# Half-width score tiles with one exponential per head, an expand moved ahead of two DMA issues, and a selection matrix in place of transposes

## The chip, the cores and the metric

The kernel runs on one core of a Trainium2 chip. The metric is the device time of one execution in microseconds. Four runs of the kernel before took 6482.04 to 6499.41 us, with a median of 6487.83 us.

## What is computed

The reference is a forward pass and its gradients. Two attention branches read the same 2048 tokens of width 576:

```python
q = (x @ wq) in 32 heads of 18;  k = x @ wk;  v = x @ wv      # branch A: one k and v for all heads
a = softmax(q k^T * 18**-0.5) v, heads joined, @ wo
mem = mem0                                                    # branch B: 64 segments of 32 tokens
for s in range(64):
    h = concat([mem, x[segment s]])                           # 8 memory rows and 32 tokens
    q, k, v = h @ Wq, h @ Wk, h @ Wv                          # 32 heads of 128
    o = softmax(masked q k^T * 128**-0.5) v, heads joined, @ Wo
    mem, out[s] = o[:8], o[8:]
b = concat(out);  g = sigmoid((x * gate_w).sum(-1))
result = g * a + (1 - g) * b
```

The outputs are this result and the gradients of ten inputs and weights for a given gradient of the result. What matters here: the memory of branch B makes its segments a chain (backward too), and branch A's scores are 2048 x 2048 for each of 32 heads, computed once in the forward half and again in the backward half.

## The kernel before, in words

The kernel is a row of stages: setup and projections, a forward weave, the bulk of branch B's attention, a backward weave, and the weight gradients at the end. The edits lie in the two weaves.

A weave (`weave`, L211) alternates, in an order that is written out by hand, one piece of branch B's chain (a Python generator, up to its next `yield`) with one step of branch A's sweep. There are 64 segments with 16 pieces each and 1024 steps, so each piece is followed by one step. No scheduler moves anything: on each engine, instructions stand in the order in which the code issues them. Every engine works through its own queue in that order and waits at the first instruction that is not ready.

**The forward sweep** is `a_pass1` (L1372). A step n handles two heads, 128 keys and 512 queries. PE gets, in this order: S of step n+1 (two matmuls with 32 rows each, `mm_S`, L1385), dP of step n (two matmuls, L1419), the accumulation of W of step n-1 (four matmuls, L1426) and of E of step n (four, L1435). ACT gets the exponential of step n+1 (`ex`, L1392), DVE gets two products W = dP * E of step n (L1424), one per head. S is one tile of two banks, held once; dP has two tiles of one bank, one per head. So S of the next step waits until ACT has read the whole S tile, and each dP waits until DVE has read the dP of the same head of the step before.

**The backward sweep** is `a_pass2` (L1499), with the same loop: `mm_S` (L1526), dP (L1548), `ex` (L1530), two products (L1553), and four accumulations of the step before, two with dS and two with E (L1561).

**The forward chain** is `b_chain_fwd` (L237). A segment's pieces are: two halves of the k projection; transpose of the memory rows of k (`mem_T`, L231, then a copy on ACT, L308); two halves of q; transpose of q (copy on DVE, L334); first half of v; scores and exponential (L342 to L353); denominators (L355 to L359); second half of v, with the normalised probabilities `c_pn` on DVE (L366) and their expansion to block form `c_PB` on POOL (L369); transpose of v; the output `po` from `c_PB` (L375 to L379), with a cast to `c_oT` on DVE (L381); and four pieces that multiply by Wo and form the next memory. POOL also issues DMAs: in the second v piece it issues the store of v's rows (`rows_out`, L364) and of `c_pn` (L367) ahead of the expansion. SP later reads v's rows back (`rows_copy`, L300).

**The backward chain** is `b_chain_bwd` (L793), 16 pieces a segment as well. It uses `mem_T` once a segment (L856), with a copy on ACT (L858). It already uses `seln` (L136, a 128x32 matrix of zeros and ones that picks the eight memory rows out of each 32) as a moving operand at L913 and L924.

`mem_T` is given rows in [128, 8, 128] with the memory rows of four groups of heads at partitions 0 to 7, 32 to 39, 64 to 71 and 96 to 103. It makes eight full 128x128 transposes into a bf16 tile and hands on a strided view of the 32 useful columns of each.

Of the kernel before, what the change touches and what calls it, by code (L numbers as in the profile page):

```python
# [6 lines left out]
ACT = mybir.ActivationFunctionType  # L7
ALU = mybir.AluOpType
AX = mybir.AxisListType
BF16 = mybir.dt.bfloat16  # L10
F32 = mybir.dt.float32
P = 128
# [13 lines left out]
SCALEA = float(DA) ** -0.5  # L26
# [4 lines left out]
class Kern:  # L31
# [197 lines left out]
        return pj  # L229

    def mem_T(self, t2, psum, tag, bufs):  # L231
        pt = psum.tile([P, 8, P], BF16, name=tag, bufs=bufs)
        for u in range(8):
            self.tr(pt[:, u, :], t2[:, u, :], P)
        return pt[:].rearrange("p u (c t) -> p u c t", t=32)[:, :, :, 0:8]

    def b_chain_fwd(self, keep, sp, psum):  # L237
        nc = self.nc
# [21 lines left out]
        def load_k(s):  # L260
            kx = sp.tile([P, HB, 32], BF16, name="c_kx", bufs=1)
            nc.sync.dma_start_transpose(kx[:], self.xtok["k"][s * 32:(s + 1) * 32, :])
            return kx
# [23 lines left out]
        for s in range(NSEG):  # L287
            h_ = hm[s % 2]
            nc.gpsimd.dma_start(self.memT_dram[:, :, s, :], h_[:, :, 0:8])
            t2 = {w: sp.tile([P, 8, E], BF16, name=f"c_{w}2", bufs=1) for w in ("k", "q", "v")}  # L290
# [6 lines left out]
            def rows_out(w):  # L297
                nc.gpsimd.dma_start(self.row_dram[w][s], t2[w][:].rearrange("p u e -> p (u e)"))

            def rows_copy(w):  # L300
                src = self.row_dram[w][s].rearrange("(c r) e -> c r e", r=32)
                t0, n = ride(s)
                nc.sync.dma_start(self.mtok[w][s * 8:(s + 1) * 8, :].rearrange("r (c e) -> c r e", c=4), src[:, 0:8, :])
                if n:
                    nc.sync.dma_start(self.xtok[w][t0:t0 + n, :].rearrange("r (c e) -> c r e", c=4), src[:, 8:8 + n, :])
# [42 lines left out]
            for u in range(8):  # L348
                for c in range(4):
                    self.mm(ps[32 * c:32 * c + 8, 64 + 8 * u:72 + 8 * u], lhsT=mT["k"][:, c, u, :],  # L350
                            rhs=qT[:, u, c, :], start=False, stop=True, tp=(0, 32 * c))
# [9 lines left out]
            proj("v", 1)  # L361
            if s + 1 < NSEG:
                kx = load_k(s + 1)
            rows_out("v")  # L364
            pn = sp.tile([P, 2, 64], BF16, name="c_pn", bufs=1)
            nc.vector.tensor_tensor(out=pn[:], in0=Et[:], in1=rd[:].unsqueeze(1).to_broadcast([P, 2, 64]), op=ALU.mult)  # L366
            nc.gpsimd.dma_start(self.pm_dram[s], pn[:].rearrange("p a b -> p (a b)"))  # L367
            PB = sp.tile([P, 16, 4, 8], BF16, name="c_PB", bufs=1)
            self.expand(PB[:], pn[:].rearrange("p a (u q) -> p (a u) q", q=8), 16)  # L369
            yield  # L370
            rows_copy("q")
            src = self.mem_T(t2["v"], psum, "c_pj", 1)
# [13 lines left out]
            if s + 1 < NSEG:  # L386
# [23 lines left out]
                for lo, hi in ((0, 256), (256, 512), (512, 576), (576, 576)):  # L410
                    if hi > lo:
                        ph = half(lo, hi)
                    if lo:
# [4 lines left out]
                        r = 64 if lo == 576 else P  # L418
# [953 lines left out]
    def a_pass1(self, keep, sp, psum, xps):  # L1372
        nc = self.nc
        T, NTT = self.T, self.NTT
        NB = NPR * (T // 512)
        dl_all = keep.tile([P, NTT, NPR, 2, 2], BF16, name="a_dl")
        QD, S, E_, W_ = {}, {}, {}, {}

        def load(b):
            if b < NB:  # L1380
                p, qb = b // 4, b % 4
                QD[b] = sp.tile([P, 512], BF16, name="a_QD", bufs=3)
                nc.sync.dma_start(QD[b][:], self.qd_dram[p][:, qb * 512:(qb + 1) * 512])

        def mm_S(n):  # L1385
            S[n] = psum.tile([P, 2, 512], F32, name="a_S", bufs=1)
            kt = n % 16
            for i in range(2):
                r = slice(32 * i, 32 * i + 32)
                self.mm(S[n][:, i, :], lhsT=self.KV[r, kt * P:kt * P + P], rhs=QD[n // 16][r, :], tp=(32 * i, 0))  # L1390

        def ex(n):  # L1392
            E_[n] = sp.tile([P, 2, 512], BF16, name="a_E", bufs=2)
            nc.scalar.activation(E_[n][:], S.pop(n)[:], ACT.Exp, scale=SCALEA)  # L1394

        def acc_mm(acc, n, src, st, first, last):
            t = src.pop(n) if src is W_ else src[n]
            for g in range(4):
                self.mm(acc[32 * g:32 * g + 32, :], lhsT=st[:, n % 16, 32 * (g % 2):32 * (g % 2) + 32],
                        rhs=t[:, g // 2, :], start=first, stop=last, tp=(0, 32 * g))  # L1400

        load(0)
        load(1)
        mm_S(0)
        ex(0)
        NP_ = 16 * NB
        acc = None
        post = None
        for n in range(NP_ + 1):
            if n < NP_:  # L1410
                kt = n % 16
                if kt == 8:
                    load(n // 16 + 2)
                if n + 1 < NP_:
                    mm_S(n + 1)
                dP = [psum.tile([P, 512], F32, name="a_dP", bufs=2) for _ in range(2)]
                for i in range(2):
                    r = slice(64 + 32 * i, 96 + 32 * i)
                    self.mm(dP[i][:], lhsT=self.KV[r, kt * P:kt * P + P], rhs=QD[n // 16][r, :], tp=(64 + 32 * i, 0))  # L1419
                if n + 1 < NP_:  # L1420
                    ex(n + 1)
                W_[n] = sp.tile([P, 2, 512], BF16, name="a_W", bufs=2)
                for i in range(2):
                    nc.vector.tensor_tensor(out=W_[n][:, i, :], in0=dP[i][:], in1=E_[n][:, i, :], op=ALU.mult)  # L1424
            if n > 0:
                acc_mm(acc, n - 1, W_, self.WK, False, n % 16 == 0)  # L1426
                if n % 16 == 0:
                    acs = sp.tile([P, 512], F32, name="a_acs", bufs=1)
                    nc.scalar.copy(acs[:], acc[:])
                    bb = n // 16 - 1  # L1430
                    post = self.a_post(bb // 4, bb % 4, acs, QD.pop(bb), sp, xps, dl_all)
            if n < NP_:
                if n % 16 == 0:
                    acc = psum.tile([P, 512], F32, name="a_acc", bufs=2)
                acc_mm(acc, n, E_, self.VK, n % 16 == 0, False)  # L1435
            if post is not None and n % 16 in (1, 4, 6):
                if next(post, "end") == "end":
                    post = None
            yield
        for _ in post:  # L1440
            pass
        for t4 in range(NTT // 4):
            ptr = xps.tile([64, 4, P], BF16, name="c_x", bufs=1)
            for j in range(4):
                self.tr(ptr[:, j, :], dl_all[:, t4 * 4 + j].rearrange("p a b c -> p (a b c)"), P)
            dlT = sp.tile([64, 512], BF16, name="a_dlT", tag="a_qt", bufs=1)
            nc.scalar.copy(dlT[:], ptr[:].rearrange("p a b -> p (a b)"))
            for p in range(NPR):
                for i in range(2):
                    nc.sync.dma_start(self.qd_dram[p][82 + 32 * i:84 + 32 * i, t4 * 512:(t4 + 1) * 512],  # L1450
                                      dlT[4 * p + 2 * i:4 * p + 2 * i + 2, :])
# [47 lines left out]
    def a_pass2(self, keep, sp, psum):  # L1499
        nc = self.nc  # L1500
# [3 lines left out]
        Q, S, E_, D_ = {}, {}, {}, {}  # L1504
# [11 lines left out]
        def pair(n):  # L1516
            return n // (NPR * NTT), n // 4, n % 4

        def mm_u(dst, n, base):
            kb, c, j = pair(n)  # L1520
            for i in range(2):
                r = slice(base + 32 * i, base + 32 * i + 32)
                self.mm(dst[i], lhsT=Q[c][0][r, j * P:j * P + P], rhs=KV[r, kb * 512:kb * 512 + 512],
                        tp=(base + 32 * i, 0))

        def mm_S(n):  # L1526
            S[n] = psum.tile([P, 2, 512], F32, name="b_S", bufs=1)
            mm_u([S[n][:, i, :] for i in range(2)], n, 0)

        def ex(n):  # L1530
            E_[n] = sp.tile([P, 2, 512], BF16, name="b_E", bufs=3)
            nc.scalar.activation(E_[n][:], S.pop(n)[:], ACT.Exp, scale=SCALEA)  # L1532

        load(0)
        load(1)
        mm_S(0)
        ex(0)
        acc = None
        NS = NPR * NTT
        NP_ = 4 * NS  # L1540
        for n in range(NP_ + 1):
# [12 lines left out]
            if n > 0:  # L1554
# [5 lines left out]
                for i4 in range(4):  # L1560
                    self.mm(acc[32 * i4:32 * i4 + 32, :], lhsT=SD[:, o % 4, 32 * i4:32 * i4 + 32],  # L1561
                            rhs=src[i4 // 2][:, i4 % 2, :],
# [236 lines left out]
```

## Time and profile before

| what | value |
|---|---|
| median of 4 runs | 6487.83 us |
| the profiled execution | 6486.87 us, of which its span is 6484.6 us |
| mean granted TensorE clock | 0.976 |
| PE busy | 5963.1 us (92% of the span) |
| DVE, ACT, POOL busy | 3772.8, 3493.8, 1962.0 us |
| forward sweep, first S to last W | 503.7 to 2456.1 us |
| backward sweep, first S to last dS | 3269.3 to 5054.4 us |
| `a_S<-...` and `b_S<-...`, 2048 matmuls each | 383 ns each |
| exponential of a whole S tile (128x1024) | 1026 and 1024 ns, 1024 of each |
| product of dP and E (128x512) | 684 and 685 ns, 2048 of each |

How to read it: the page gives busy times per engine and per group of instructions (line, engine, output tile <- input tiles). The order in time gives the start of each instruction and the idle time before it with what ended it; rows that follow each other on one engine are merged ("x2"), and then the length is that of all of them from the first start to the last end. PE overlaps matmuls, so one that is still in flight counts as busy while the next one waits. PE's starts are therefore more telling than its busy time.

### The profile page before, as it was taken

The numbers are of one execution on the slowest core, as the hardware profiler recorded it, in microseconds if no ns is written. First come the engines' busy times: TensorE is split into PE (matmuls) and PEld (weight loads), VectorE is DVE, ScalarE is ACT, GpSimd is POOL, SyncE is SP. The second block draws the span as 40 slices with busy tenths as digits, with TensorE's granted clock in tenths as the row PEclk, the third lists the DMA queues.
The fourth block names the chain that finished last, engine by engine and source line by source line (L and its number), as shares of the span: only waits on it lengthen the run. The fifth ranks groups of instructions, "written<-read, shape, count | busy, mean of one in ns | idle before, by whom it ended". The sixth has DMA issues, their size and how long they took to land. (4 is left out here: it accounts for less than half of the span.)

```text
span 6484.6 us, 208625 instructions
## 1 busy us (share of the span) xinstructions
PE 5963.1 (92%) x88611; PEld 3364.2 (52%) x88822; DVE 3772.8 (58%) x7061; ACT 3493.8 (54%) x5105; POOL 1962.0 (30%) x3451
## 2 busy tenths in 40 slices
PE   7898999999999994999969999999999899899996
PEld 5443444444444443877734444444444677675443
DVE  4336777777777773666658888888888211111111
ACT  3326777777777773666547777777677322211101
POOL 3003333333333333444423333333333111112212
PEclk9999999999999997999989999999999999999998
DMA  4636656556564435999864343433444799896643
GB/s 152 225 148 113 118 117 116 120 116 117 120 114 103 101 78 148 258 255 257 248 202 102 99 99 102 103 100 101 103 102 102 196 241 249 228 284 205 219 149 111
DMA packets 1368109, 991.95 MB, mean 153 GB/s; under 512 B 931613, under 2 KB 1184806, under 8 KB 1356486
## 3 DMA queue, kind: packets, MB, share of 16 engines
q1 hardware_dynamic: 1285030, 780.53, 49.1%
q0 software_dynamic: 82144, 198.05, 9.7%
q8 instruction: 696, 11.40, 0.7%
q14 instruction: 239, 1.96, 0.1%
HBM read 552.41 MB, written 384.76 MB: 145 GB/s over the span
## 5 line engine op out<-in xcount | busy, mean ns | idle before, releaser
L1424 DVE TENSOR_TENSOR a_W<-a_dP,a_E 128x512 bf16<-128x512 f32 x2048 | 1315.7, 684 | 464.1 <-PE a_dP L66 428.9
L1553 DVE TENSOR_TENSOR b_dS<-b_dP,b_E 128x512 bf16<-128x512 f32 x2048 | 1316.3, 685 | 322.1 <-PE b_dP L66 239.7
L1532 ACT ACTIVATE b_E<-b_S 128x1024 bf16<-128x1024 f32 x1024 | 1048.9, 1024 | 505.9 <-PE b_dP L66 357.0
L1394 ACT ACTIVATE a_E<-a_S 128x1024 bf16<-128x1024 f32 x1024 | 1050.9, 1026 | 170.2 <-PE a_dP L66 157.8
L66 PE MATMUL b_dP<-b_KV,b_QD 32*128 32x512 bf16 x2048 | 595.5, 380 | 5.5 <-DVE b_dS L1553 5.3
L66 PE MATMUL b_S<-b_KV,b_QD 32*128 32x512 bf16 x2048 | 399.8, 383 | 102.9 <-ACT b_E L1532 51.3
L66 PE MATMUL a_dP<-a_QD,l_KV 32*128 32x512 bf16 x2048 | 489.7, 382 | 0.9 <-DVE a_W L1424 0.7
L66 PE MATMUL w_acc<-w_d,w_h 128*128 128x512 bf16 (+1 forms) x2352 | 471.0, 379 | 2.5
L66 PE MATMUL r_pj<-WT,r_dT 128*32 128x288 bf16 x12288 | 443.9, 286 | 0.0
L66 PE MATMUL a_S<-a_QD,l_KV 32*128 32x512 bf16 x2048 | 398.7, 383 | 45.8 <-ACT a_E L1394 43.5
L66 PE MATMUL a_acc<-a_W,l_WK 128*32 128x512 bf16 x4096 | 409.8, 390 | 0.1
L66 PE MATMUL b_acc<-b_dS,b_SD 128*32 128x512 bf16 x2048 | 403.9, 391 | 0.0
L66 PE MATMUL b_acc<-b_E,b_SD 128*32 128x512 bf16 x2048 | 403.4, 391 | 0.0
L66 PE MATMUL a_acc<-a_E,l_VK 128*32 128x512 bf16 x4096 | 398.7, 379 | 0.0
L66 PEld LDWEIGHTS <-r_dT 128*32 128x32 bf16 x12288 | 328.7, 97 | 77.9 <-issue 0.3
L1027 DVE COPY y_T<-y_pt 128x512 bf16<-128x512 bf16 x256 | 97.2, 420 | 463.1 <-PE y_pt L71 463.1
L66 PEld LDWEIGHTS <-w_h 128*128 128x128 bf16 (+1 forms) x2400 | 212.9, 100 | 244.7 <-issue 3.4
L66 PEld LDWEIGHTS <-b_SD 128*32 128x32 bf16 x4096 | 105.1, 92 | 432.2 <-issue 431.2
L66 PEld LDWEIGHTS <-hm 128*32 128x32 bf16 x7680 | 206.3, 97 | 226.9 <-issue 14.3
L66 PEld LDWEIGHTS <-b_QD 32*128 32x128 bf16 x4096 | 140.4, 91 | 306.6 <-issue 215.3
L1013 ACT CAST y_tdk<-y_pk 128x512 bf16<-128x512 f32 x128 | 75.1, 587 | 377.4 <-PE y_pk L66 222.2
L66 PEld LDWEIGHTS <-l_WK 128*32 128x32 bf16 x4096 | 105.2, 92 | 325.4 <-issue 325.3
(412 smaller groups left out, 11650.3 us busy)
## 6 DMA issues: line engine op xcount, KB each, us to landing
b_QD<-qd_dram SPq DMA_DIRECT2D x256, 128.0 KB
b_SD<-sd_dram SPq DMA_DIRECT2D x256, 128.0 KB
dOx_dram<-p_tok SPq DMA_DIRECT2D x16, 1024.0 KB
c_vx<-vx_dram SPq DMA_DIRECT2D x256, 64.0 KB
krow_dram<-c_k POOLq DMA_DIRECT2D x64, 256.0 KB, 2.6
qrow_dram<-c_q POOLq DMA_DIRECT2D x64, 256.0 KB, 2.8
vrow_dram<-c_v POOLq DMA_DIRECT2D x64, 256.0 KB, 3.1
x_q<-qx_dram SPq DMA_DIRECT2D x32, 512.0 KB
```

What stands on the lines that cost most here:

```text
L66: return self.nc.tensor.matmul(out, lhsT, rhs, start=start, stop=stop, tile_position=tp, skip_group_check=True)
L1013: nc.scalar.copy(d[w][:, r, :], pk[:])
L1027: nc.vector.tensor_copy(T_[t][w][:], pt[:])
L1394: nc.scalar.activation(E_[n][:], S.pop(n)[:], ACT.Exp, scale=SCALEA)
L1424: nc.vector.tensor_tensor(out=W_[n][:, i, :], in0=dP[i][:], in1=E_[n][:, i, :], op=ALU.mult)
L1532: nc.scalar.activation(E_[n][:], S.pop(n)[:], ACT.Exp, scale=SCALEA)
L1553: nc.vector.tensor_tensor(out=D_[n][:, i, :], in0=dP[i][:], in1=E_[n][:, i, :], op=ALU.mult)
```

## The change

It has three parts.

1. In both sweeps, S becomes two tiles of one bank (one per head, from a pair of buffers under one name), and the exponential becomes two instructions, one per head, that write the two halves of the same E tile. The PSUM space is the same: two banks.
2. `mem_T` becomes eight matmuls with the rows as stationary operand and `seln` as moving operand (128x32), into an f32 tile, in place of eight transposes into a bf16 tile. The 32 columns of each block are now contiguous.
3. In the second v piece of the forward chain, POOL's expansion of `c_PB` comes ahead of the two DMA issues, and the store of `c_pn` ahead of the store of v's rows.

```diff
     def mem_T(self, t2, psum, tag, bufs):
-        pt = psum.tile([P, 8, P], BF16, name=tag, bufs=bufs)
+        pt = psum.tile([P, 8, 32], F32, name=tag, bufs=bufs)
         for u in range(8):
-            self.tr(pt[:, u, :], t2[:, u, :], P)
-        return pt[:].rearrange("p u (c t) -> p u c t", t=32)[:, :, :, 0:8]
+            self.mm(pt[:, u, :], lhsT=t2[:, u, :], rhs=self.seln[:].rearrange("p c q -> p (c q)"))
+        return pt[:].rearrange("p u (c t) -> p u c t", t=8)
...
             proj("v", 1)
             if s + 1 < NSEG:
                 kx = load_k(s + 1)
-            rows_out("v")
             pn = sp.tile([P, 2, 64], BF16, name="c_pn", bufs=1)
             nc.vector.tensor_tensor(out=pn[:], in0=Et[:], in1=rd[:].unsqueeze(1).to_broadcast([P, 2, 64]), op=ALU.mult)
-            nc.gpsimd.dma_start(self.pm_dram[s], pn[:].rearrange("p a b -> p (a b)"))
             PB = sp.tile([P, 16, 4, 8], BF16, name="c_PB", bufs=1)
             self.expand(PB[:], pn[:].rearrange("p a (u q) -> p (a u) q", q=8), 16)
+            nc.gpsimd.dma_start(self.pm_dram[s], pn[:].rearrange("p a b -> p (a b)"))
+            rows_out("v")
             yield
...
         def mm_S(n):
-            S[n] = psum.tile([P, 2, 512], F32, name="a_S", bufs=1)
+            S[n] = [psum.tile([P, 512], F32, name="a_S", bufs=2) for _ in range(2)]
             kt = n % 16
             for i in range(2):
                 r = slice(32 * i, 32 * i + 32)
-                self.mm(S[n][:, i, :], lhsT=self.KV[r, kt * P:kt * P + P], rhs=QD[n // 16][r, :], tp=(32 * i, 0))
+                self.mm(S[n][i][:], lhsT=self.KV[r, kt * P:kt * P + P], rhs=QD[n // 16][r, :], tp=(32 * i, 0))
 
         def ex(n):
             E_[n] = sp.tile([P, 2, 512], BF16, name="a_E", bufs=2)
-            nc.scalar.activation(E_[n][:], S.pop(n)[:], ACT.Exp, scale=SCALEA)
+            for i, t in enumerate(S.pop(n)):
+                nc.scalar.activation(E_[n][:, i, :], t[:], ACT.Exp, scale=SCALEA)
...
         def mm_S(n):
-            S[n] = psum.tile([P, 2, 512], F32, name="b_S", bufs=1)
-            mm_u([S[n][:, i, :] for i in range(2)], n, 0)
+            S[n] = [psum.tile([P, 512], F32, name="b_S", bufs=2) for _ in range(2)]
+            mm_u([t[:] for t in S[n]], n, 0)
 
         def ex(n):
             E_[n] = sp.tile([P, 2, 512], BF16, name="b_E", bufs=3)
-            nc.scalar.activation(E_[n][:], S.pop(n)[:], ACT.Exp, scale=SCALEA)
+            for i, t in enumerate(S.pop(n)):
+                nc.scalar.activation(E_[n][:, i, :], t[:], ACT.Exp, scale=SCALEA)
```

## The prediction

> **What bounds the kernel now.** I read the slices of the page first, then the busy times of the stages, then PE, ACT and DVE in order of time through one segment of each woven stage, then the waits. The edits touch two stages only: the forward weave (about 505 to 2450 us) and the backward weave (about 3340 to 5055 us). The busy times by stage (length, then PE, PEld, DVE, ACT, POOL):
>
> ```profile
> 505.00:2450.00 1945.00, 1867.53 (x33926) 879.72 (x33926) 1428.47 (x2547) 1425.97 (x1974) 692.74 (x1404) 1.00 0.55 110
> ...
> 3340.00:5150.00 1810.00, 1715.07 (x31811) 866.49 (x31811) 1424.52 (x2532) 1231.99 (x1536) 589.98 (x1021) 0.99 0.43 107
> ```
>
> PE looks full, DVE and ACT are three quarters full, the granted clock is 1.00. But a waiting PE with a matmul still in flight counts as busy, so the bound has to be read from the order of the steps. Each weave has 64 segments of 16 steps. In a step PE issues two S matmuls, two dP matmuls, the accumulations and one piece of the chain. ACT, DVE and PE at the end of one forward segment (start, length, in brackets the idle time before and what ended it):
>
> ```profile
> 1508.81 1.02 ACT L1394 ACTIVATE a_E<-a_S 128x1024 bf16<-128x1024 f32 x1
> ...
> 1508.92 1.29 DVE L1424 TENSOR_TENSOR a_W<-a_dP,a_E 128x512 bf16<-128x512 f32 x2 [0.25 <-PE a_dP L66]
> ...
> 1508.39 0.59 PE L66 MATMUL a_dP<-a_QD,l_KV 32*128 32x512 bf16 x2
> ...
> 1509.89 0.39 PE L66 MATMUL a_S<-a_QD,l_KV 32*128 32x512 bf16 x2 [0.15 <-ACT a_E L1394]
> 1509.90 0.73 PE L66 MATMUL a_dP<-a_QD,l_KV 32*128 32x512 bf16 x2
> ```
>
> Two loops stand in these rows. **The exponential loop**: S issues, ACT starts 0.48 later (4021.40 to 4021.88 in the backward weave), takes 1.02, and the next S issues 0.05 after its end (1509.83 to 1509.89): 1.55 us. **The product loop**: the first dP issues (1508.39), DVE starts 0.53 later (1508.92), two products take 1.29 (end 1510.21), and the second dP of the next step issues 0.05 later: the dP pair lasts 0.73 where one takes 0.37 to 0.39, so its second half began at 1510.26. That is 0.53 + 1.29 + 0.05 = 1.87 us from a first dP to the next step's second dP.
>
> Walking a forward segment (1478 to 1510 us) from second dP to second dP, nine steps are PE's own work (1.91 to 2.27 us) and seven are the product loop, 1.87 less the distance between the two dP of the step before. The exponential loop sets S in five forward and nine backward steps, but PE then stands at the second dP until DVE is done. So the product loop, not the exponential loop, ends last in nearly all steps that PE does not fill.
>
> **The change part by part.**
>
> *Expand ahead of the two DMA issues.* POOL around 1500 us:
>
> ```profile
> 1499.80 0.61 POOL L298 DMA_DIRECT2D vrow_dram<-c_v  x1
> 1500.41 0.54 POOL L367 DMA_DIRECT2D pm_dram<-c_pn  x1
> 1500.96 1.09 POOL L205 TENSOR_TENSOR c_PB<-c_pn,bmask 128x512 bf16<-128x512 bf16 x1
> ```
>
> and PE's waits in the forward weave (total, times, longest):
>
> ```profile
> PE a_S L66 <- ACT a_E L1394: 42.3, 190, 1.1
> PE c_x L66 <- POOL c_PB L205: 32.2, 60, 1.4
> ```
>
> PE waits 0.52 for c_PB at 1502.10. c_pn is done at 1498.80 and POOL is free at 1499.71 (end of a_qt), so c_PB would be ready at 1500.80, before PE comes to it at about 1501.58: the wait goes, with 0.8 to spare. What is late next is the product loop. The second dP moves from 1502.60 to DVE's end at 1502.30 plus 0.05, a gain of 0.25. S itself moves 0.5 ahead, so the following product pair starts when the c_oT cast (0.42, straight after 1502.30) ends, about 1502.64, and is done before PE comes back 1.73 later. So that step's stand of 0.12 at the second dP goes too: 0.25 + 0.12 = 0.37 us a segment. Moved behind the expand are the two DMA issues: the vrow issue goes from 1499.80 to about 1501.35, lands a median 3.0 us later, and SP reads those rows from 1507.17, so 2.8 us remain; the vmT issue behind them stays at about 1501.95. Cost nothing; if that cover were gone, SP's in-order queue would wait, and the next vx load with it.
>
> *Exponential per head.* The whole takes 1.024 us. A 128x512 exponential from PSUM is in the trace (L623, 597 ns), and the next ACT instruction starts 0.49 after it:
>
> ```profile
> 3064.25 0.60 ACT L623 ACTIVATE x_E<-x_S 128x512 bf16<-128x512 f32 x1 [0.19 <-issue]
> 3064.74 0.27 ACT L624 ACTIVATE x_E<-x_m 128x128 bf16<-128x128 f32 x1
> ```
>
> A pair is then 0.493 + 0.597 = 1.090, **0.066 more** than the whole; without any overlap 1.194, 0.17 more (the upper end). I take 0.066, since both halves are ready together when PE is not waiting. The Trainium skill ("ScalarE: Activation LUTs", What ACT_TABLE_LOAD costs) gives an instruction 186 ns plus 0.833 ns an element, with back-to-back ones overlapping by about 93 ns. By it an added one is an estimated 93 ns, where these rows make it 66; the sum below would be some 4 us worse by it.
>
> What the halves buy: the first S needs only the first exponential, about 0.5 earlier. But the matmuls issue in order, S0, S1, dP0, dP1, and S1 needs the second exponential. So where S waits for ACT, dP0 is not earlier in that step: it is 0.066 later. Only a following step can gain, if it waits for ACT as well, because ACT can start it sooner. What 0.066 costs depends on what follows. Before a step that PE fills: nothing. Before a step of the product loop: 0.066, once.
>
> Forward: such pairs are two a segment (the S at 1494.99, whose next step is the product loop; and the one at 1500.48, before the step that loses the PB wait). 2 x 0.06 = 0.12 lost. Backward, from 4006.7 on, the same bookkeeping: the S at 4008.27 comes 0.07 later, so the dP1 at 4010.14 does; the step after absorbs it (S at 4011.42 is 0.06 later, but the S at 4009.87 was not); the next has it again; from the transposes at 4015.53 to the end of the segment it is carried through. The early S0 shortens only steps whose dP1 waits for DVE anyway. Net +0.07 us a segment. The waits added on ACT's results by the second S have only dP and the accumulations behind them, which wait already. The changed program also lets the first matmul after each of the new products' tiles wait for PE itself; those products end at least a step before, so I take nothing for it.
>
> *Selection matrix.* Eight transposes take 0.40 from first to last issue (1499.67, 0.62 in all less the last one's 0.22); eight 128x32 products 0.19 (0.025 apart in c_x<-c_PB). Some 0.21 of PE, and about 0.04 of the gap to S, for 256 calls: 64 us if PE were the bound. It is not there: the forward steps with the q and v calls and the backward one are product-loop steps, and their S waits for ACT. Only the k call's step, where dP1 is 0.09 behind DVE instead of 0.05, gains 0.04. The c_qT copy reads f32 instead of bf16: 0.42 as c_oT instead of 0.29, and 0.17 of DVE idle behind it (1491.55 to 1491.72) hides the 0.13; uncovered it would be 64 x 0.13 = 8 us. ACT's copies do not change (373 ns from bf16, 366 from f32).
>
> *Sum.* Forward: 63 x (-0.37 + 0.12 - 0.04) = -18 us. Backward: 64 x 0.07 = +4 us. Together -14 on the profiled execution's 6486.87 us (span 6484.6): **6473 us**. That execution is 1 us under the median of 6487.83, so the sum is used as it is.
>
> **The rivals.**
>
> *The sweeps start to pipeline.* S follows a piece's last matmul by 0.31 after a projection, 0.15 after transposes, 0.11 after 128x32 products when nothing is waited for; what is over that is waiting for ACT, about 0.8 us a segment forward and 1.45 backward. All of it gained is 64 x 2.25 = 144, 6487 - 18 - 144 = 6325; half is about 6400. For it: ACT's waits for PE before an exponential are 156 and 324 us in the two stages. Against: dP0 stands behind S1. Chance 0.22.
>
> *Slower: the 0.066 is paid in every step where S waits for ACT.* There are 5 + 9 = 14 a segment, 64 x 14 x 0.066 = 59, less the gain with no delay, 63 x 0.41 = 26: **6520 us**. It decides from about six such steps a segment on (64 x 0.066 x 6 = 25). For it: dP0 is later in each. Against: in most, the next dP1 is fixed by PE. Without overlap (0.17) it would be 6613. Chance 0.20.
>
> *Hidden.* The wait for c_PB goes, but another takes its whole place (c_oT, or SP): 6485. Chance 0.10.
>
> **How the numbers follow.** My forecast has 0.48. A measurement of this kernel can tell about 0.2% (13 us) from no change, and 6473 lies just beyond that edge, so I count 0.33 of it as faster and 0.15 as the same. With the rivals: faster 0.33 + 0.22 = 0.55, same 0.15 + 0.10 = 0.25, slower 0.20. The forecast's own range is 6455 to 6494: the gain of 0.37 whole with no delay at the lower end (-26, a little more if the selection matrix helps), the pair at 1.194 at the upper end (forward 63 x (-0.41 + 0.34) = -4, backward 64 x 0.17 = 11). Signs are mixed, so the range reaches half-way into both rivals: 6400 to 6520.
>
> **What would show it.** Right: c_PB gone from PE's waits and the second dP of that step 0.25 earlier; L623-like halves of 0.60 with 0.49 between starts; ACT busier by some 70 us a weave; the forward weave about 18 us shorter and the backward one about 4 longer; 8 products in 0.19. Wrong: a backward weave shorter by tens of us (dP is then not held by S1), halves that do not overlap, or a new wait of PE for c_oT, or of SP for vrow.

## The result, and the profile after

The changed kernel takes 6498.08 us (median of 34 runs, 6485.98 to 6508.73) where the kernel before takes 6488.24 us (median of 52 runs, 6478.18 to 6500.8). The ratio is **1.0013, 95% interval 1.0008 to 1.0018**: 8 us slower by the ratio, 10 by the medians, where 14 us less was forecast. The size lies inside the band of 0.2% that was called the same, the sign is the other one. The profiled execution took 6489.4 us (span 6487.6), near the fast end of the kernel's runs and only 2.5 us over the profiled one of the kernel before, at a mean granted clock of 0.973 where the one before had 0.976. The rows below account for these 2.5 us; the other 6 to 7 lie in executions without a profile.

The busy times by stage of the kernel after (length, then PE, PEld, DVE, ACT, POOL, granted clock, DMA share, GB/s):

```profile
505.00:2440.00 1935.00, 1919.38 (x33938) 857.36 (x33937) 1423.32 (x2549) 1468.30 (x2997) 686.40 (x1405) 1.00 0.56 111
3340.00:5150.00 1810.00, 1780.58 (x31518) 850.06 (x31515) 1412.31 (x2509) 1236.23 (x2508) 582.26 (x1011) 0.98 0.42 106
```

The forward window is chosen ten microseconds shorter and holds the same work, with some 40 us more of ACT. In the backward weave the granted clock has gone from 0.99 to 0.98, which will matter below. By first and last instruction, the forward sweep went from 1953.1 us (first S to the end of the last W) to 1940.8, the stretch between the sweeps from 812.5 to 808.3, and the backward sweep from 1785.8 to **1804.4**. So the loss is in the backward weave: 18.6 us where 4 were forecast.

PE's wait for c_PB is gone. POOL and PE around one expand of the kernel after:

```profile
1496.76 1.06 POOL L205 TENSOR_TENSOR c_PB<-c_pn,bmask 128x512 bf16<-128x512 bf16 x1
1497.77 0.61 POOL L368 DMA_DIRECT2D pm_dram<-c_pn  x1
1498.38 0.54 POOL L298 DMA_DIRECT2D vrow_dram<-c_v  x1
...
1498.67 0.19 PE L66 MATMUL c_x<-c_PB,c_vx 128*128 128x32 bf16 x1
```

c_PB is ready at 1497.82 and PE comes to it 0.85 later; the prediction had 0.8. In the list of waits of the forward weave c_PB is left only as POOL's own wait for c_pn:

```profile
DVE a_W L1425 <- PE a_dP L66: 405.2, 667, 2.1
...
ACT a_E L1395 <- PE a_dP L66: 96.7, 184, 0.8
...
POOL c_PB L205 <- DVE c_pn L365: 8.0, 2, 7.7
```

The wait of a_S for ACT has shrunk in the list as well (42.3 us before, 0.7 now), but not in the kernel. S0 now issues by itself, and while it is in flight the profile counts PE as busy although S1 stands behind the second exponential. The groups show it: a_S is busy 486.8 us instead of 398.7 for the same matmuls, and ACT's halves are the 0.60 that L623 had promised. They make ACT some 70 us busier in each weave, as forecast (1116.7 and 1119.9 us, where the whole tiles took 1048.9 and 1050.9):

```profile
L1534 ACT ACTIVATE b_E<-b_S 128x512 bf16<-128x512 f32 x2048 | 1116.7, 600 | 511.0 <-PE b_dP L66 457.4
L1395 ACT ACTIVATE a_E<-a_S 128x512 bf16<-128x512 f32 x2048 | 1119.9, 604 | 108.4 <-PE a_dP L66 97.5
```

Two steps of the backward weave of the kernel after, in order of time:

```profile
3987.85 0.39 PE L66 MATMUL b_S<-b_KV,b_QD 32*128 32x512 bf16 x2
3987.86 0.39 PE L66 MATMUL b_dP<-b_KV,b_QD 32*128 32x512 bf16 x2
...
3988.27 1.08 ACT L1534 ACTIVATE b_E<-b_S 128x512 bf16<-128x512 f32 x2 [1.17 <-PE b_dP L66]
3988.41 1.29 DVE L1555 TENSOR_TENSOR b_dS<-b_dP,b_E 128x512 bf16<-128x512 f32 x2 [0.72 <-PE b_dP L66]
3989.00 0.78 PE L66 MATMUL b_S<-b_KV,b_QD 32*128 32x512 bf16 x2
...
3989.41 0.71 PE L66 MATMUL b_dP<-b_KV,b_QD 32*128 32x512 bf16 x2
```

ACT starts 0.42 after the first S (0.48 before), but DVE starts 0.55 after the first dP, where the product loop of the prediction had 0.53. In the second step S0 goes out at 3989.00, S1 only at about 3989.40, and dP behind it.

**The usual step.** For every step I took the time from its second dP to that of the step before, and the median over the segments. The medians repeat within 1 or 2 ns between kernels where nothing is changed, so a table of them shows each part's effect on each step. Step k of a segment follows piece k: forward, step 2 follows the transpose of k and step 11 the output from c_PB; backward, step 4 follows the transpose of r_dOm. In ns (the steps left out move by 3 ns at most in the kernels of these tables):

```text
forward      2    3    5    7    8   10   11   12   13   14   all 16 steps
before    1905 1952 1866 1866 1679 1867 1924 1866 2273 1866   30439
after     1893 1938 1893 1892 1699 1893 1699 1733 2288 1894   30197
backward     0    1    2    3    4    5    6    8   10   12   15   all 16
before    1551 1606 1552 1605 1551 1689 1646 1748 1867 1867 1866   27338
after     1510 1674 1511 1673 1510 1475 1886 1775 1893 1894 1893   27482
```

A usual segment is 0.242 us shorter forward and 0.144 longer backward: 63 x -0.242 = -15.2 and 64 x 0.144 = +9.2 us. What a sweep takes from its second segment on over its usual steps (rare long steps) was 2.8 us forward and 10.1 backward before, and is 5.5 and **19.9** after. So about half of the backward loss is in rare steps. Most of it has one look; the clock in three stretches of the kernel after, then the products of r_dOm ahead of the middle one and the rows with which it begins:

```profile
4030.00:4035.00 5.00, 5.00 (x58) 1.49 (x57) 4.39 (x8) 4.38 (x10) 1.80 (x4) 1.00 0.17 53
4036.00:4042.00 6.00, 6.00 (x72) 2.27 (x68) 3.51 (x8) 2.97 (x6) 1.69 (x2) 0.50 0.74 109
4042.50:4048.00 5.50, 5.48 (x109) 2.80 (x105) 4.34 (x8) 3.90 (x9) 1.17 (x3) 1.00 0.09 26
```

```profile
4033.45 0.37 PE L66 MATMUL r_x<-seln,r_dOm 128*128 128x32 bf16 x8
...
4035.83 0.61 PE L66 MATMUL b_S<-b_KV,b_QD 32*128 32x512 bf16 x2
4035.84 0.61 PE L66 MATMUL b_dP<-b_KV,b_QD 32*128 32x512 bf16 x2
```

From 4035.83 on, for 5.7 us, a score matmul takes 0.61 instead of 0.39; by its record the granted clock is 0.50 from 4035.65 to 4042.47, 6.8 us. Six such stretches lie in the backward sweep, in segments 7, 8, 27, 43, 59 and 60, each beginning with the second pair of S behind the small products of r_dOm (4035.83, the products are at 4033.45); each costs 1.81 to 1.86 us, 11.1 together. Two shorter ones (2.1 us, 3.4 by the record) at the end of a segment cost 0.8 each. The kernel before has only the stretch near the start of the sweep that all kernels of this study have.

### The profile page after: what moved, and what is told of

Read it like the earlier page. It is cut to its first block, busy times and chain, and to the rows that moved or that the text cites. A ratio compares the mean times of both kernels' runs of the same rounds, so it can differ in the third digit from the quotient of the medians.

```text
span 6487.6 us, 212656 instructions
## 1 busy us (share of the span) xinstructions
PE 6103.3 (94%) x88611; PEld 3335.0 (51%) x88822; DVE 3767.5 (58%) x7061; ACT 3551.6 (55%) x7153; POOL 1951.8 (30%) x3451
## 4 chain that ended last, share of the span: by engine, by line
PE 82%; issue 7%; DMA 5%; SPq 2%; ACT 2%; POOL 1%; DVE 1%; another core or an unknown queue 0%; POOLq 0%; ACTq 0%; DVEq 0%
PE w_acc L66 10%; PE r_pj L66 8%; PE c_pj L66 8%; PE a_acc L66 8%; PE b_S L66 7%; PE a_S L66 6%; PE b_acc L66 5%; PE p_pb L66 4%; PE r_x L66 3%; PE b_dP L66 3%; PE c_x L66 3%; PE x_tr L71 2%; DMA dsx_dram<-x_dS 2%; PE a_dP L66 2%; PE y_pdx L66 2%
## 5 line engine op out<-in xcount | busy, mean ns | idle before, releaser
L1534 ACT ACTIVATE b_E<-b_S 128x512 bf16<-128x512 f32 x2048 | 1116.7, 600 | 511.0 <-PE b_dP L66 457.4
L1395 ACT ACTIVATE a_E<-a_S 128x512 bf16<-128x512 f32 x2048 | 1119.9, 604 | 108.4 <-PE a_dP L66 97.5
L66 PE MATMUL b_S<-b_KV,b_QD 32*128 32x512 bf16 x2048 | 516.7, 388 | 35.4 <-DMA b_QD<-qd_dram 32.5
L66 PE MATMUL a_dP<-a_QD,l_KV 32*128 32x512 bf16 x2048 | 511.8, 381 | 2.6 <-DVE a_W L1425 1.1
L66 PE MATMUL a_S<-a_QD,l_KV 32*128 32x512 bf16 x2048 | 486.8, 382 | 11.4 <-DMA a_QD<-qd_dram 1.1
L66 PE MATMUL a_acc<-a_E,l_VK 128*32 128x512 bf16 x4096 | 398.7, 379 | 0.0
```

The source lines that it names most:

```text
L66: return self.nc.tensor.matmul(out, lhsT, rhs, start=start, stop=stop, tile_position=tp, skip_group_check=True)
L1395: nc.scalar.activation(E_[n][:, i, :], t[:], ACT.Exp, scale=SCALEA)
L1534: nc.scalar.activation(E_[n][:, i, :], t[:], ACT.Exp, scale=SCALEA)
```

## The experiments

Theory: (1) the expand gives what was forecast; (2) S0, released by itself, sends one more signal from PE and makes the product loop 0.026 longer, and dP stands behind S1; (3) the small products of r_dOm leave TensorE too little to do and let the clock fall. Rivals: the pair of exponentials is the cost; the clock falls because of the halves.

**One part at a time.** `e_pb`, `e_sel` and `e_half` are the kernel before with part 3, 2 and 1 of the change alone (the diff is that of the change). `e_two_exp` keeps the whole score tile:

```diff
-            nc.scalar.activation(E_[n][:], S.pop(n)[:], ACT.Exp, scale=SCALEA)
+            Sn = S.pop(n)
+            for i in range(2):
+                nc.scalar.activation(E_[n][:, i, :], Sn[:, i, :], ACT.Exp, scale=SCALEA)
```

What was expected of `e_pb`:

> The kernel before with one part of the change alone: the expand of c_PB ahead of the two POOL DMA issues. In the changed kernel the forward steps at the expand (the three steps around it) are together 0.31 us a segment shorter than before, while the other forward steps are longer. Theory: the expand alone is worth about 0.31 to 0.37 us x 63 segments = 20 to 23 us, all of it in the forward weave, and the other forward steps do not change. Rival (hidden): another wait takes its place once nothing else changes, and the time stays within 5 us of before. The backward weave should not change under either.

Of `e_sel`:

> The kernel before with the products with the selection matrix alone. By the step bookkeeping of the changed kernel they are worth at most 0.04 us a segment forward and nothing backward: 0 to -3 us. But the changed kernel's trace holds eight more stretches of about 5.7 us in the backward weave in which matmuls take 0.61 instead of 0.39 us (granted clock 0.50), each costing about 1.6 us, and they begin near the steps of r_x<-seln,r_dOm and r_dx. Theory A: the smaller products leave TensorE less active there and bring these stretches; then this kernel shows several of them in the backward weave, and its time is 5 to 15 us over before. Theory B: the halves bring them; then this kernel shows none beyond the one near 3305 us that the kernel before has, and its time is 0 to 3 us under before.

Of `e_half`:

> The kernel before with the half-width score tiles and an exponential per head alone. Theory (signals): with S0 released to ACT by itself, the four matmuls S0, S1, dP0, dP1 that issue together send one signal more, and DVE starts its product 0.553 us after the first dP instead of 0.527, as in the changed kernel; five forward and four backward product-loop steps a segment are 0.026 longer, and S waiting for two exponentials does the rest: forward +0.13 us x 64 = +8, backward +0.14 x 64 = +9, together about +18 us. Rival (paid in every ACT-waiting step): 14 x 0.066 x 64 = +59 us. Rival (nothing): within 5 us of before, and the loss of the changed kernel comes from elsewhere. On the half-rate stretches of the clock: under theory A none more than before; under theory B about eight more and some +12 us beyond the 18.

Of `e_two_exp`:

> The kernel before with its whole two-bank score tile, but two exponentials of one bank each in place of one of both: the added ACT instruction without the early release of S0 and without the added signal. Theory (signals): DVE's product starts 0.527 after the first dP as before; ACT takes about 1.09 instead of 1.02, and every S that waits for ACT comes 0.066 later; where the step behind is a product-loop step this is paid: about one or two steps forward and three or four backward a segment, 64 x 0.066 x 5 = about +20 us. If the added signal were not the cause of the 0.026, this kernel would show 0.553 as well. If it is no slower than before, then the added instruction costs nothing and the halves' loss is the signal and the order alone.

Measured against the kernel before in the same job (6505.69 us):

| kernel | median, us | ratio, 95% interval | usual segment forward, backward, ns | rare long steps forward, backward, us |
|---|---|---|---|---|
| e_pb | 6491.19 | 0.9980 (0.9971 to 0.9989) | -363, -6 | 19.1, 9.7 |
| e_sel | 6512.38 | 1.0011 (1.0002 to 1.0020) | -57, -10 | 12.8, 15.8 |
| e_half | 6524.83 | 1.0033 (1.0020 to 1.0045) | +120, +135 | 2.7, 14.4 |
| e_two_exp | 6506.80 | 1.0004 (0.9996 to 1.0013) | +59, +7 | 5.8, 11.5 |

```text
forward      2    3    5    7    8   10   11   12   13   14   all 16 steps
e_pb      1906 1952 1866 1866 1679 1866 1679 1733 2288 1866   30076
e_sel     1867 1938 1866 1866 1680 1866 1918 1866 2274 1866   30382
e_half    1906 1952 1892 1891 1700 1892 1891 1892 2274 1893   30559
e_two_exp 1907 1952 1866 1866 1743 1866 1918 1865 2274 1867   30498
backward     0    1    2    3    4    5    6    8   10   12   15   all 16
e_sel     1551 1606 1550 1605 1551 1482 1852 1748 1865 1865 1864   27328
e_half    1512 1672 1510 1673 1510 1728 1633 1772 1891 1892 1890   27473
e_two_exp 1565 1593 1564 1593 1563 1674 1660 1748 1865 1865 1865   27345
```

*The expand.* Steps 11 and 12 lose 245 and 133 ns, step 13 gains 15: 0.363 a segment, forecast 0.37. It should give 23 us and gave 13 (0.2%): in the profiled execution rare steps cost 16 us more than before. One case in `e_pb`, a row and then the stretch behind it:

```profile
781.64 0.21 PE L66 MATMUL c_pj<-WoN,c_oT 128*32 128x64 bf16 x2 [1.52 <-issue]
```

```profile
784.60:790.30 5.70, 5.70 (x73) 1.95 (x72) 2.44 (x5) 3.20 (x6) 1.51 (x2) 0.72 0.55 67
```

PE stands 1.52 us for nothing that the profile shows, and then the granted clock is 0.72 in the mean for 5.7 us. Four such spells with half clock in them cost 11.7 us in this execution, and `e_sel` has five forward that cost 7.8. With both edits together (`e_pb_sel`, below) none has half clock, so they are not the price of either in every build; why they fell here was not tried.

*The halves.* Steps 5, 7, 10, 12 and 14 forward and 8, 10, 12 and 15 backward are 21 to 27 ns longer, in line with one signal, and the kernel is 19 us slower where about 18 were expected. DVE starts 0.553 after the first dP (median); one such step of `e_half`:

```profile
4013.97 0.49 PE L66 MATMUL b_dP<-b_KV,b_QD 32*128 32x512 bf16 x2
4014.39 1.08 ACT L1534 ACTIVATE b_E<-b_S 128x512 bf16<-128x512 f32 x2 [1.12 <-PE b_dP L66]
...
4014.53 0.69 DVE L1555 TENSOR_TENSOR b_dS<-b_dP,b_E 128x512 bf16<-128x512 f32 x1 [0.48 <-PE b_dP L66]
```

With two exponentials on the whole tile it is 0.527 as before, and the steps named are unchanged. A step of `e_two_exp`:

```profile
4014.63 0.39 PE L66 MATMUL b_S<-b_KV,b_QD 32*128 32x512 bf16 x2 [0.34 <-ACT b_E L1536]
4014.64 0.67 PE L66 MATMUL b_dP<-b_KV,b_QD 32*128 32x512 bf16 x2
4015.05 1.08 ACT L1536 ACTIVATE b_E<-b_S 128x512 bf16<-128x512 f32 x2 [0.21 <-PE b_dP L66]
4015.16 1.29 DVE L1557 TENSOR_TENSOR b_dS<-b_dP,b_E 128x512 bf16<-128x512 f32 x2 [0.28 <-PE b_dP L66]
```

So the 0.026 belongs to the early release of S0, not to the second ACT instruction. The Trainium skill ("TensorE: Matmul & The Clock Gate", The cost: per-tile semaphore tail) says that matmuls that finish together signal one after the other, 26.3 ns each; 0.553 less 0.527 is 26 ns, and the rows agree.

My expectation for `e_two_exp`, +20 us, missed. The exponential does take 1.08 instead of 1.02, but ACT starts 0.42 to 0.43 after S instead of 0.48 (4014.63 to 4015.05), so the exponential loop is only some 0.01 longer. It is paid once a segment, in forward step 8 (+64), and comes to nothing backward, where it moves between neighbouring steps.

*The selection products.* Forward they give 0.057 a segment. Backward, step 5 gets 207 ns shorter and step 6 206 longer: all of it goes back in the next step, where PE stands at the product loop. And the clock: `e_sel` has three of the stretches of 5.6 us behind r_dOm, `e_half` none of that kind but five of at most 2.3 us at the end of a segment, 0.8 to 1.3 us each. One of `e_sel`:

```profile
3478.00:3483.00 5.00, 4.62 (x73) 1.52 (x69) 4.42 (x9) 4.15 (x6) 2.00 (x4) 1.00 0.21 55
3483.60:3489.20 5.60, 5.53 (x74) 2.26 (x71) 3.31 (x7) 2.42 (x3) 1.69 (x2) 0.50 0.77 119
```

So the long stretches come with the products, as theory A has it, and short ones come with the halves.

**The halves taken away, and the order of S and dP.** `e_pb_sel` is the changed kernel without part 1. `e_dp_first` is that with dP ahead of S in both sweeps, `e_after_dp_first` the changed kernel with the same edit. It is, forward (backward alike):

```diff
-                if n + 1 < NP_:
-                    mm_S(n + 1)
                 dP = [psum.tile([P, 512], F32, name="a_dP", bufs=2) for _ in range(2)]
...
                 if n + 1 < NP_:
+                    mm_S(n + 1)
                     ex(n + 1)
```

Expected of `e_pb_sel`:

> The changed kernel without the halves: the expand ahead of the DMA issues and the selection products, with the whole score tile and one exponential. In the single-part runs a usual forward segment was 0.36 us shorter with the expand and 0.06 shorter with the products, and 0.12 longer with the halves; a usual backward segment was 0.13 longer with the halves and unchanged without them. Theory (usual steps add up): this kernel's usual forward segment is about 0.4 us shorter than before's and its backward one the same, so 64 x 0.4 = 25 us less; what half-rate stretches of the clock and PE's waits for no visible cause add (10 to 20 us more than before in the single-part runs) comes off that: 10 to 25 us under before. Rival: these additions eat the whole gain, and it is within 5 us of before.

Of `e_dp_first`:

> The kernel of the expand and the selection products with the whole score tile, and in both weaves the two dP matmuls of a step are issued ahead of the two S matmuls of the next. Theory (dP stands behind S): the first dP no longer waits for the exponential and is not third in the row of signals, so DVE starts about 0.48 to 0.50 after it instead of 0.527; each product-loop step is 0.03 to 0.05 shorter and S, which has over 0.4 us to spare in most steps, costs nothing by coming later: seven forward and about nine backward steps a segment, 64 x 16 x 0.04 = some 40 us less than without it, at least 15. Rival (exponential late): S now stands behind the second dP, which waits for DVE, so ACT starts later, the product loop becomes a loop of both engines, and the kernel is slower than before by tens of us.

Of `e_after_dp_first`:

> The changed kernel with its halves, and the two dP matmuls of a step issued ahead of the two S matmuls of the next in both weaves. Theory (dP stands behind S): as for the whole tile, DVE starts about 0.48 to 0.50 after the first dP instead of 0.553, since S0's and S1's signals now follow instead of leading; the loss of 0.13 us a segment backward and 0.12 forward goes and more is gained: 64 x 14 x 0.06 = some 50 us under the changed kernel, at least 20. If the loss came from the pair of exponentials itself, it stays: within 10 us of the changed kernel.

Measured, against 6490.04 us:

| kernel | median, us | ratio, 95% interval | usual segment forward, backward, ns | rare long steps, us |
|---|---|---|---|---|
| e_pb_sel | 6465.33 | 0.9964 (0.9951 to 0.9978) | -417, -1 | 5.8, 13.6 |
| e_dp_first | 6451.98 | 0.9939 (0.9926 to 0.9951) | -681, -72 | 8.0, 11.1 |
| e_after_dp_first | 6450.42 | 0.9939 (0.9926 to 0.9951) | -698, -83 | 7.6, 13.5 |

Parts 2 and 3 alone are worth 0.36%, about what their usual segments add up to. dP first gives another quarter of a per cent, 13 us by the medians, less than the 40 us expected and just short of the 15 named as the least, since part of what a step gains is given back in the next. With the halves it gives the 50 us under the changed kernel that were expected (48 by the ratios). Two steps of `e_dp_first`:

```profile
4013.23 0.39 PE L66 MATMUL b_dP<-b_KV,b_QD 32*128 32x512 bf16 x2
4013.24 0.39 PE L66 MATMUL b_S<-b_KV,b_QD 32*128 32x512 bf16 x2
...
4013.73 2.51 DVE L1551 TENSOR_TENSOR b_dS<-b_dP,b_E 128x512 bf16<-128x512 f32 x4 [0.96 <-PE b_S L66]
...
4014.47 0.37 PE L66 MATMUL b_dP<-b_KV,b_QD 32*128 32x512 bf16 x1
4015.07 0.37 PE L66 MATMUL b_dP<-b_KV,b_QD 32*128 32x512 bf16 x1 [0.23 <-DVE b_dS L1551]
```

DVE starts 0.49 to 0.50 after the first dP where it had to wait for it, and the next first dP goes out at 4014.47 while DVE still works, so DVE makes four products without a pause. The halves are now neither loss nor gain: both ratios are 0.9939. What they cost in the changed kernel was thus the place of dP behind S, in the order of issue and of signals, and not the pair of exponentials.

**The clock.** `e_after_rtr` is the changed kernel with eight transposes for r_dOm alone; `e_after_sel2` issues the eight products of r_dOm twice instead (`mem_T_tr` is `mem_T` as it was before; the second part of the diff is the body of a copy of the new `mem_T`, called for r_dOm only):

```diff
-            src = self.mem_T(dOm, psum, "r_x", 1)
+            src = self.mem_T_tr(dOm, psum, "r_x", 1)
...
-        for u in range(8):
-            self.mm(pt[:, u, :], lhsT=t2[:, u, :], rhs=self.seln[:].rearrange("p c q -> p (c q)"))
+        for u in range(16):
+            self.mm(pt[:, u % 8, :], lhsT=t2[:, u % 8, :], rhs=self.seln[:].rearrange("p c q -> p (c q)"))
```

Expected of `e_after_rtr`:

> The changed kernel, but the backward chain's r_dOm is transposed by eight transposes as in the kernel before; the forward selection products stay. In the changed kernel six stretches of 5.7 us at half clock begin just behind r_x<-seln,r_dOm and cost 1.85 us each, 11 us in all, and the products gave the backward weave's usual segment nothing. Theory A (the lighter products leave TensorE too little active there): these six go, the backward weave is about 8 to 11 us shorter than in the changed kernel, and what is left at half clock are the short ones of 0.8 to 1.2 us that the halves alone showed. Rival B (the stretches come from the halves or from chance): as many of them as in the changed kernel, time within 3 us of it.

Of `e_after_sel2`:

> The changed kernel, but the eight selection products of r_dOm in the backward chain are issued twice over into the same tile: TensorE does 0.19 us more work there a segment, and nothing else changes. With eight transposes in their place the six stretches of 5.7 us at half clock were gone. Theory (too little work on TensorE in that step brings the half clock): with the work doubled they go as well, or nearly, and the backward weave is 5 to 10 us shorter than the changed kernel's although it does more. Rival (something in the kind of matmul, or in the order of time, brings them): about as many as in the changed kernel, and the backward weave the same or up to 64 x 0.19 = 12 us longer.

Measured: 6484.28 us, ratio 0.9994 (0.9985 to 1.0002), and 6483.69 us, 0.9993 (0.9985 to 1.0002), each to the kernel before; the changed kernel has 1.0013 (1.0008 to 1.0018), and the intervals do not touch. In both, the long stretches behind r_dOm are gone, four short ones that cost 0.8 to 0.9 us each are left, the rare steps of the backward sweep cost 10.6 and 10.4 us instead of 19.9, and that sweep takes 1795.4 and 1794.8 us instead of 1804.4. Their usual backward segments are those of the changed kernel (27476, 27472 and 27482 ns): the work that was put back costs nothing and keeps the clock up. Over all runs with a profile, kernels with the eight light products in that step show 6, 3, 2, 3 and 0 long stretches (the changed kernel, `e_sel`, `e_pb_sel`, `e_after_dp_first`, `e_dp_first`), the seven others in which the step is heavier show none, the filled kernels below aside.

Where the step falls in time counts as well. In every execution half clock sets in at times that are whole multiples of 3.413 us apart. All 14 long stretches set in 0.13 to 0.37 us ahead of the first dP of step 5. Counting the segments that have such a moment 0.1 to 0.4 us ahead of that dP: in the five kernels with the light products there are 26, and 14 of them fall to half clock there; in the seven others there are 42, 7 of them in `e_after_sel2`, and none does. `e_dp_first` has one and `e_best` (below) none, so their zeros tell nothing. That TensorE's work in this step decides is thus shown by the doubled products at the same moments; how much work is enough was not measured, nor why 12 of the 26 keep the full clock. The short stretches set in at the end of a segment, in the four kernels that have halves with S ahead of dP (2, 5, 4 and 4) and once in `e_best`; `e_after_dp_first`, with halves and dP first, has none, though its segments meet the same moments, so they are not a price of halves as such.

The Trainium skill ("TensorE: Matmul & The Clock Gate", Part 1: The HAM clock gate) says that the array falls to half of its clock after an idle window of about 3.4 us, that these windows run on by themselves, and names idle gaps of that length as the case to avoid. The runs agree on the half (0.50) and on the length (3.413 us from one possible moment to the next), but here no gap of that kind stands ahead of the stretch at 4035.83: in the ten microseconds ahead of it PE issues a matmul at least every 0.37 us. The page also tells of a second case, with short idles between groups of matmuls; that is nearer to this one.

**What the runs point to.** `e_best` is `e_dp_first` with the transposes kept for r_dOm. `e_best_fill` also puts the accumulations that are ready between the two dP (forward the four with a_E, backward three), and `e_fill_half` is that with halves:

```diff
                 for i in range(2):
                     r = slice(64 + 32 * i, 96 + 32 * i)
                     self.mm(dP[i][:], lhsT=self.KV[r, kt * P:kt * P + P], rhs=QD[n // 16][r, :], tp=(64 + 32 * i, 0))
+                    if i == 0:
+                        acc_mm(acc, n, E_, self.VK, n % 16 == 0, False)
```

Expected of `e_best`:

> What the runs so far point to: the kernel before with the expand ahead of the DMA issues, the selection products in the forward chain only (eight transposes stay for r_dOm), the whole score tile with one exponential, and dP ahead of S. Expected: the usual segments of the version with all the selection products (forward 29.76 us, backward 27.27), no stretch of 5.7 us at half clock behind r_dOm: 0.6% under before, some 40 us, within 6 us of the version with all the products. If the half clock were only moved elsewhere, its long stretches would show in other steps and it would be no faster than 0.5% under before.

Of `e_best_fill`:

> The same, and between the first and the second dP of a step PE issues the accumulations that it can already do (forward the four with a_E, backward the two with b_E and the first with b_dS). With dP ahead of S, PE still stands 0.2 to 0.6 us between the two dP in seven forward and eight backward steps of a segment, waiting for DVE's second product. Theory (PE's stand is what is left in these steps): up to 0.2 us of PE's work goes into each stand, 64 x 15 x 0.1 to 0.2 = 100 to 190 us less than without it, if DVE is not the bound by then; at least 30. Rival (the product loop of DVE alone sets these steps): within 10 us of the version without it.

Of `e_fill_half`:

> The same as the filled version, with the half-width score tiles and an exponential per head. With dP ahead of S, halves and whole tile were equal (0.9939 of before each), since S no longer stands ahead of dP. Where the fill makes the steps shorter, the exponential loop (whole: 0.48 + 1.02 + 0.05 = 1.55 us) may bind, and then the halves would pay at last: 10 to 40 us under the filled version with the whole tile. If the steps stay above 1.55 us or DVE binds, the two are equal within 10 us.

Measured, against 6489.61 us: `e_best` 6446.49 us, **0.9937 (0.9925 to 0.9950)**, faster than both kernels, with no long stretch behind r_dOm (but `e_dp_first` had none either, and no segment of `e_best` was at the moment where one sets in, so the transposes' share in it is not shown). `e_best_fill` 7204.19 us, 1.1098 (1.1082 to 1.1114), and `e_fill_half` 7164.13 us, 1.1044 (1.1029 to 1.1060): the theory of the fill fails, and so does its rival. Rows of `e_best_fill`, and then of the kernel before:

```profile
3999.89 0.38 PE L66 MATMUL b_dP<-b_KV,b_QD 32*128 32x512 bf16 x1
...
4000.20 0.39 PE L66 MATMUL b_acc<-b_E,b_SD 128*32 128x512 bf16 x2
...
4000.53 0.39 PE L66 MATMUL b_dP<-b_KV,b_QD 32*128 32x512 bf16 x1
4000.53 0.39 PE L66 MATMUL b_S<-b_KV,b_QD 32*128 32x512 bf16 x2
4000.85 0.39 PE L66 MATMUL b_acc<-b_dS,b_SD 128*32 128x512 bf16 x1
```

```profile
4001.05 0.39 PE L66 MATMUL b_dP<-b_KV,b_QD 32*128 32x512 bf16 x2
4001.37 0.39 PE L66 MATMUL b_acc<-b_dS,b_SD 128*32 128x512 bf16 x2
4001.38 0.39 PE L66 MATMUL b_acc<-b_E,b_SD 128*32 128x512 bf16 x2
4001.59 1.16 PE L66 MATMUL r_pj<-WT,r_dT 128*32 128x288 bf16 x32
```

dP uses 32 rows of the array, the accumulations all 128. Matmuls on different rows start 3 to 4 ns apart, so the four of S and dP go as one group. From a group to the next of the other kind, start to start, it is 0.31 to 0.32 us (3999.89, 4000.20, 4000.53, 4000.85); from one to the next of the same kind 0.216 as a median (4001.38 to 4001.59 here), so the change of kind itself costs some 0.1. The fill splits the group of four in two and puts the accumulations between. That is 0.315 + 0.322 in place of one 0.216, 0.42 us more, and the seven forward steps that PE fills (0, 1, 3, 4, 6, 9 and 13) are indeed 0.42 to 0.43 longer. The other steps, which had room, grow by 0.09 to 0.55, and the usual forward segment from 29759 to 34933 ns. Backward, half clock sets in at the end of 36 of the segments besides, and the usual step 0 alone grows from 1411 to 3218 ns.

`e_fill_half` is 40 us faster than `e_best_fill`, as its theory had it, but not by the halves: the usual forward segments are equal (34958 and 34933), and the whole-tile one has 38 us of rare steps forward, nearly all at half clock.

## Why the prediction was wrong

- *The loops.* Right: the product loop sets the steps that PE does not fill. Their medians follow it (1.866 us before, 1.893 with the halves, 1.830 with dP first): its constant 0.53 is what the halves moved (to 0.55) and dP first moved the other way (to 0.49).
- *The expand ahead of the DMA issues*: -0.37 forecast, -0.363 measured alone.
- *The selection matrix*: forward -0.04 forecast, -0.057 measured; the longer c_qT copy is hidden as said (the steps behind it do not move). Backward "nothing" held for the usual step, but **this term failed**: "It is not there" counts only PE's time. Fewer columns also mean less work for TensorE, and the clock answers to it: 11.1 us in the profiled execution, the largest single miss of the sum.
- *Exponential per head, the pair*: the halves overlap as forecast (0.60 and 0.49), but ACT starts 0.05 earlier after S, so the 0.066 is nearly all made up. The estimate of 93 ns by the Trainium skill ("ScalarE: Activation LUTs", What ACT_TABLE_LOAD costs) would have been further off, by 5 us in the sum (0.027 in 2 x 63 + 64 places; the prediction says 4): the pair takes 0.06 more.
- *Exponential per head, forward*, +0.12: the changed kernel's steps 5, 7, 8, 10, 11 and 14 are 20 to 28 ns longer than with the expand alone, 0.147 together. The size is near by luck, the cause is another: five or six signals, and not two delays of 0.06.
- *Exponential per head, backward*, "Net +0.07 us a segment": **this step failed too**. It is 0.144, for the added signal sits in every product loop behind a step in which the four matmuls issue together (steps 8, 10, 12, 15, and once in each pair of the steps 0 to 3). The prediction looked at when the first S may issue, and not at what its signal delays.
- *Sum*: by usual segments -15.2 and +9.2, together -6; the rare steps add 12.5 over before (2.7 forward, 9.8 backward) and turn the sign; the stretch between the sweeps, where nothing was edited, gives 4 back in this execution. That is some 2 us more, and the two profiled executions differ by 2.5. The medians are 8 to 10 us apart, and what makes up the rest is open. The light products of r_dOm are a likely part: taking them out is worth 12 us by the ratios (1.0013 and 0.9994), and 9 in the profiled sweeps.
- *The rivals.* The sweeps did not pipeline; dP does stand behind S1. The 0.066 is not paid in every step that waits for ACT: `e_two_exp` paid 0.4 ns a step backward. No other wait takes c_PB's place. The slower side came by a mechanism that was not among them.

## What to carry to other kernels

Where one engine issues in order, an earlier release buys nothing for what is queued behind a later one, and the signal that it adds delays what matters; put first what the slowest loop waits for. Before making TensorE's work smaller in a stage that other engines bound, look at the granted clock of short stretches, not at its mean. Price an edit by medians of single steps and add the rare long steps separately: here each of the two had about half of the backward sweep's loss.

## What the runs showed that was not expected

- Each signal ahead, from matmuls that issue together, delays those behind: from the first dP to DVE it is 0.492 us with none ahead, 0.527 with one and 0.553 with two.
- With S ahead of dP, an exponential of one bank starts 0.42 to 0.43 us after S, one of two banks 0.48, also where the tile is whole (`e_two_exp`).
- Half clock for 5.7 us after a step with 0.2 us less of matmuls in it, with no long idle time of PE; the same products issued twice, none of these stretches. It sets in only at moments 3.413 us apart, so a profile in which no light step meets such a moment does not show it.
- From matmuls on 32 rows to matmuls on 128 rows, or back, it is 0.31 to 0.32 us from start to start, where the same kind follows after 0.216; splitting one pair of dP in this way made the kernel 11% slower.
